# An attention and MLP kernel whose MLP moves from four batches of 448 tokens to runs of 256, 512, 512 and 512 tokens

## The chip, the cores and the metric

The kernel runs on one core of one Trainium2 chip. The metric is the time of one execution on the device in microseconds (us); the time before is the median of three runs. The profile and the trace are of one such execution, taken by the hardware profiler.

## What is computed

Four batches of 12 heads, 448 tokens, head width 64. Softcap attention, then an MLP of 768 to 2048 to 768 on the 1792 tokens:

```python
scores = matmul(q, k.transpose(0, 1, 3, 2)) / sqrt(64)      # (4, 12, 448, 448)
scores = cap * tanh(scores / cap)
attn = exp(scores - max); attn = attn / (sum(attn) + 1e-9)
x = matmul(attn, v).transpose(0, 2, 1, 3).reshape(1792, 768)
h = x @ w_in                                                # (1792, 2048)
out = maximum(0.01 * h, h) @ w_out                          # (1792, 768)
```

q, k, v are float32. w_in and w_out arrive as 8-byte floats and are made into float32 on the chip.

## The kernel before

**Layout.** Everything lies transposed: features on the 128 partitions, tokens along the free dimension. Attention goes by 24 pairs of heads (`plan_pair`, six pairs to a batch); a pair gives one 128-row block of x for the 448 tokens of its batch. The MLP goes by units (`plan_unit`), 34 to a batch: 16 "l1" units, each one 128-row block f of g = leak(h) from the six blocks of x, and 18 "l2" units, each one of six output blocks e from one of three chunks (6, 5, 5 blocks) of g. So each of the four batches has 576 MLP matmuls of 448 columns (line 639).

**Three products for one.** Operands of the MLP are split in a high float32r part and a low rest (`split`, lines 237 to 244: a cast on ScalarE or VectorE and a subtraction on VectorE or GpSimd). A block product is three float32r matmuls: high by high, high by low, low by high. This holds for the weights (each unit's 768 or 640 columns are split again in each batch, line 635), for x (`xh`, `xl`), and for g (`gh`, `gl`). The scores are single float32 matmuls in the first 8 pairs (`fs=8`, lines 481 and 485) and three float32r ones from then on ("parted", lines 475 and 478). The product with v (line 490) is float32 always.

**Weights.** In the first batch each unit's raw 8-byte words are loaded by SP into one of three `wr` buffers, made into float32 in one of three `ws` buffers by two ScalarE steps (lines 624 and 626) and two VectorE steps (628 and 631), stored to a scratch tensor by SP (line 634), and split into one of four `w` buffers. Later batches load `ws` from scratch (line 610) and split.

**Second product.** An l2 unit fills a bank `m` (two banks) with one chunk's product; the first chunk is copied to an accumulator `acc` (line 686), the next two are added on VectorE (line 688); then it is transposed (line 696) and stored.

**Row sums of attention.** Pairs from `tv=4` on are "late": VectorE transposes and reduces `t` (lines 553 and 554) and a small matmul (line 558) folds; the earlier ones use a matmul with ones (line 494).

**Order.** All steps go into a planner (`Plan`). `issue` takes them one by one: the step that can start first by the planner's own costs, ties by a rank. Ranks come from the pair (10 per pair), the unit (`off`, `step`) and many hand-kept shifts (`role`, `pair`, `unit`). Engines run what they get in that fixed order.

Of the kernel before, what the change touches and what calls it, by code (L numbers as in the profile page):

```python
# [22 lines left out]
    kT=2,  # L23
    qT=2,
    pf=6,
    t=1,
    nx=2,
    x=11,
    wr=3,
    ws=3,  # L30
    w=4,
    g=11,
    wl=15,
    wp=6,
    al=7,
    dp=1,
    tv=4,
    fs=8,
    td=1,
# [3 lines left out]
    ps=2.5,  # L43
    pp=7,
    pn=14,
    k1=2,
    wu=16,
    capr=0.5,
    psp=0.05,
    role={'x fold': -295.81, 'x fixed_vx': -299.23, 'x regs': -42.87, 'x cap dma': -211.23, 'x inv': 315.25, 'pair kraw.0 dma zero': -546.92, 'pair qraw.0 zero': -219.17, 'pair kT.0 zero': 57.73, 'pair qT.0 zero': -71.66, 'pair vc.0 dma zero': -347.94, 'pair kb.0 zero': 51.96, 'pair sc.0 zero': -62.66, 'pair sc.1 zero': -60.67, 'pair sc.2 zero': -103.79, 'pair sc.3 zero': -298.93, 'pair pf.0 zero': -156.85, 'pair pf.1 zero': -205.87, 'pair pf.2 zero': -157.62, 'pair pf.3 zero': -489.26, 'pair t.0 zero': -166.0, 'pair po.0 zero': -272.22, 'pair po.1 zero': 319.75, 'pair sums.0 zero': -198.54, 'pair x.0 zero': 43.72, 'pair rt.0 zero': -114.98, 'pair sums.1 zero': -286.23, 'pair x.1 zero': -187.35, 'pair xh.0 zero': -62.77, 'pair xl.0 zero': 379.14, 'pair kraw dma first': -17.18, 'pair qraw dma first': 25.25, 'pair kT first': 241.28, 'pair qT first': 119.93, 'pair vc dma first': -13.95, 'pair kb first': -4.45, 'pair sc first': 21.61, 'pair pf first': -5.02, 'pair t first': -5.18, 'pair po first': 7.52, 'pair sums first': 9.58, 'pair x first': -33.84, 'pair rt first': -21.66, 'pair xh first': -48.48, 'pair xl first': -46.92, 'pair tT first': 13.32, 'pair rs first': -188.37, 'pair tot first': -369.34, 'pair kraw dma': 35.73, 'pair qraw dma': 242.02, 'pair kT': 6.6, 'pair qT': 203.27, 'pair vc dma': 74.48, 'pair kb': 2.15, 'pair sc': -22.89, 'pair pf': 5.21, 'pair t': 8.02, 'pair po': 41.21, 'pair tT': 30.3, 'pair rs': 5.92, 'pair tot': 21.32, 'pair rt': 9.24, 'pair sums': -3.2, 'pair x': -40.44, 'pair xh': -9.56, 'pair xl': 1.21, 'pair kh': -8.73, 'pair kw': -13.73, 'pair qh': 3.89, 'pair qw': -112.56, 'pair fixed_kb': 95.84, 'pair kp': 5.63, 'unit wr dma first': -2.28, 'unit raw first': 0.27, 'unit ws first': -2.37, 'unit scratch dma first': 3.41, 'unit whi first': -11.34, 'unit wlo first': 1.32, 'unit m first': -1.57, 'unit g first': -3.96, 'unit gh first': -19.01, 'unit gl first': -35.21, 'unit acc first': -15.22, 'unit ot first': -312.25, 'unit store dma first': -392.77, 'unit ws dma': -136.88, 'unit whi': -55.41, 'unit wlo': 24.55, 'unit m': -6.45, 'unit g': 9.41, 'unit gh': 273.06, 'unit gl': -123.62, 'unit acc': -15.09, 'unit ot': -213.65, 'unit store dma': -297.05, 'unit kraw': 383.71, 'unit qraw': 313.76, 'unit store': 380.48},  # L50
    pair=[-97.5, -29.54, -10.01, -81.08, -2.56, -7.22, -8.28, 1.67, -3.12, -0.55, -2.65, 1.08, 17.61, 8.32, -39.21, 410.26, -40.91, -16.81, -14.87, 33.57, 95.16, 115.18, 129.54, -71.79],
    unit=[-0.28, -0.21, -0.88, 6.67, -264.45, 3.41, -2.63, -0.84, -1.84, 0.28, 20.81, -3.53, 3.55, -3.25, -1.64, -47.01, -7.36, 5.17, 3.91, -103.33, 4.51, 3.09, -61.42, -11.89, 1.54, -48.36, 9.33, -68.08, -27.04, -5.27, 26.68, -113.13, -88.2, -10.05, 12.8, -156.6, -2.11, -183.67, -162.47, 158.92, -22.97, -152.48, -6.03, -72.99, -38.37, 254.26, 19.64, 15.97, 28.61, 138.2, -309.66, -31.27, -337.13, -7.5, -131.59, 50.82, -44.43, -139.65, 109.84, 27.93, -30.49, -5.42, -7.75, 17.18, -21.48, 90.32, -101.6, 89.32, 60.62, 111.39, -80.62, 162.65, 58.43, 84.77, -48.48, 134.44, 59.07, -210.52, -67.16, 9.79, 12.21, -194.14, -122.58, -150.52, 53.64, -14.13, -35.26, -6.88, 39.73, -132.0, -235.15, -94.07, -115.95, -149.66, -84.77, -83.37, -63.71, -192.65, 151.45, 304.04, 143.0, 46.16, 106.2, 131.92, -65.0, 11.79, 13.3, 34.01, 91.68, 46.33, 129.93, 85.49, 88.82, -179.59, -95.4, 173.17, -320.42, -171.98, -148.32, -76.07, -10.55, 124.57, 325.93, 137.64, 19.88, -79.55, -273.53, 127.53, -258.11, -46.13, -1.94, 80.33, 90.56, -124.12, -123.41, 174.91],
    off=[70, 73, 67, 70],
    step=[1.65, 1.35, 1.65, 1.875],
    pen=0.05,
    pend=0.8,
    phases=[(40.0, {'pool': 1.54, 'dve': 0.21, 'pe': 46.39}), (100.0, {'pool': 0.2, 'dve': 0.47, 'act': 0.31, 'pe': 31.15, 'sp': 28.36}), (200.0, {'pool': 0.53, 'dve': 1.21, 'act': 0.5, 'pe': 6.99}), (1000000000.0, {'pool': 0.78, 'dve': 0.74, 'act': 0.94, 'sp': 11.31})],
    ev=24,
# [7 lines left out]
class Plan:  # L66
# [9 lines left out]
    SWITCH = 20  # L76
# [91 lines left out]

@with_exitstack
def softcap_attention_mlp(  # L170
# [21 lines left out]

    keep = ctx.enter_context(tc.tile_pool(name="keep", bufs=1))
# [7 lines left out]

    def ring(tag, n, shape, dt=F32, pool=const):
        plan.ring(tag, n)
        row = []
        for i in range(n):
            t = pool.tile(shape, dt, name=f"{tag}_{i}", tag=f"{tag}_{i}")
            row.append(t)
        tiles[tag] = row
# [43 lines left out]

    ring("kraw", T["raw"], [P, NB, 32])
    ring("qraw", T["raw"], [P, NB, 32])
    for tag in ("kT", "qT"):
        row = []
        for j in range(2):
            t = const.tile([P, S], F32, name=f"{tag}_{j}", tag=f"{tag}_{j}")
            row.append(t)
        alias(tag, row, [i % 2 if i < T["fs"] else 0 for i in range(B * NP)])  # L260
    ring("kb", 2, [P, P])

# [3 lines left out]
    plan.ring("kp", 1)  # L266
    plan.ring("kw", 1)
    plan.ring("qw", 1)
    block = lambda w: successor(f"kb_{'hl'.index(w)}", [P, P], F32R)
    plan.ring("fixed_kb", 1)  # L270
    ring("vc", 2, [P, 8, D])
    ring("sc", 2, [P, 2, 512], F32, psum)
    late_pair = lambda i: i >= T["tv"]
    n_pairs = B * NP
    two_banks = [psum.tile([P, 512], F32, name=f"po_{j}", tag=f"po_{j}") for j in range(2)]

    alias("po", two_banks, [-1 if late_pair(v // 2) and v % 2 else (v // 2) % 2 if late_pair(v // 2) else v % 2 for v in range(2 * n_pairs)])
# [145 lines left out]
    def plan_pair(i):  # L423
# [426 lines left out]
```

## Time and profile before

| | us |
|---|---|
| median of 3 runs (680.1 to 680.89) | 680.81 |
| span of the profiled execution | 677.4 |
| PE busy | 648.0 |
| VectorE (DVE) busy | 517.1 |
| ScalarE (ACT) busy | 367.0 |
| GpSimd (POOL) busy | 183.4 |

The profiled execution is one of the program; its span runs from the first to the last instruction, and the median of the runs is 3.4 us longer. A busy PE is one with a matmul in flight; it may still be slowed by what it waits for. The views used are: busy time by stretch, groups of instructions, the chain that ended last, and the order in time. The first MLP matmul starts 55 us after the span's start, and the last of batch 0's 576 ends near 246 us; these two times cut the stretches.

### The profile page before, as it was taken

What the parts mean: (1) busy time and instruction counts of PE and PEld (TensorE: products, weight loads), DVE (VectorE), ACT (ScalarE), POOL (GpSimd) and SP (SyncE); (2) the same over time, 40 slices, a digit from 0 to 9 for tenths busy, and PEclk for the clock granted to TensorE, in tenths of its full rate; (3) what the DMA queues carried; (4) which work ended last, traced back from release to release, by engine and by line L of the source; (5) the groups of instructions that cost most, each with busy time, mean ns of one, the idle gap of its engine ahead of it and who ended that gap; (6) DMA issues with size and microseconds to landing.
All of it is one profiled execution on the core that took longest, in us unless ns stands there. A gap on an engine that the chain in (4) does not pass through costs nothing.

```text
span 677.4 us, 9303 instructions
## 1 busy us (share of the span) xinstructions
PE 648.0 (96%) x3208; PEld 510.2 (75%) x3208; DVE 517.1 (76%) x773; ACT 367.0 (54%) x586; POOL 183.4 (27%) x191
## 2 busy tenths in 40 slices
PE   7999999999998999999999999999999999999993
PEld 3334678786765787888656798699879799999993
DVE  3899999999999999538488877954686577465652
ACT  3999998796879843437397614822443113222120
POOL 7425242424633273101266420110011202000001
PEclk8999999999998999999999999999999999999998
DMA  9969899977877677334263355343222266233324
GB/s 134 229 108 223 211 278 233 304 228 200 236 224 219 157 192 155 116 98 118 52 149 79 81 141 119 107 117 102 84 92 78 78 168 156 74 122 108 104 51 73
DMA packets 160104, 98.23 MB, mean 145 GB/s; under 512 B 116529, under 2 KB 141105, under 8 KB 160049
## 3 DMA queue, kind: packets, MB, share of 16 engines
q1 hardware_dynamic: 154192, 91.70, 52.6%
q0 software_dynamic: 3072, 5.51, 4.1%
q10 hardware_dynamic: 2784, 0.34, 0.4%
q8 instruction: 27, 0.44, 0.3%
q14 instruction: 29, 0.23, 0.1%
HBM read 79.43 MB, written 18.09 MB: 144 GB/s over the span
## 4 chain that ended last, share of the span: by engine, by line
PE 62%; DVE 23%; ACT 5%; issue 4%; DMA 3%; POOL 1%; SPq 1%; DVEq 0%; POOLq 0%; ACTq 0%
PE m L639 53%; PE po L490 5%; DVE wr L628 4%; DVE ws L631 3%; PE sc L478 3%; DVE w L244 2%; DMA qraw<-in_q_dram 2%; ACT pf L513 1%; DVE late L679 1%; ACT pf L515 1%; DVE gl L244 1%; DVE t L527 1%; DVE qT_second L244 1%; PE sc L475 1%; DMA wr<-in_moe_w_out_dram 1%
## 5 line engine op out<-in xcount | busy, mean ns | idle before, releaser
L639 PE MATMUL m<-xh,w 128*128 128x448 f32 x768 | 229.9, 372 | 3.4 <-DVE w L244 3.4
L639 PE MATMUL m<-gh,w 128*128 128x448 f32 x768 | 229.3, 369 | 3.9 <-DVE late L688 1.4
L639 PEld LDWEIGHTS m<-xh,w 128*128 128x128 f32 x768 | 144.8, 189 | 24.7 <-DVE w L244 5.5
L639 PEld LDWEIGHTS m<-gh,w 128*128 128x128 f32 x768 | 144.1, 188 | 25.3 <-issue 6.4
L639 PE MATMUL m<-xl,w 128*128 128x448 f32 x384 | 141.1, 367 | 0.0
L639 PE MATMUL m<-gl,w 128*128 128x448 f32 x384 | 140.6, 366 | 0.2 <-DVE gl L244 0.2
L237 ACT CAST w<-ws 128x768 fp32r<-128x768 f32 (+1 forms) x95 | 75.5, 796 | 113.0 <-PE m L639 85.0
L244 DVE TENSOR_TENSOR w<-ws,w 128x768 fp32r<-128x768 f32 (+1 forms) x120 | 114.4, 956 | 19.8 <-ACT w L237 17.8
L513 ACT ACTIVATE pf<-sc 128x896 f32<-128x896 f32 (+1 forms) x90 | 70.7, 823 | 18.2 <-PE sc L478 7.4
L393 POOL DMA_DIRECT2D qraw<-in_q_dram x92 | 58.3, 640 | 74.4 <-DVE gh L241 37.4
L639 PEld LDWEIGHTS m<-xl,w 128*128 128x128 f32 x384 | 72.6, 189 | 6.1 <-issue 0.4
L639 PEld LDWEIGHTS m<-gl,w 128*128 128x128 f32 x384 | 72.1, 188 | 6.3 <-DVE gl L244 0.5
L515 ACT ACTIVATE pf<-pf 128x896 f32<-128x896 f32 (+1 forms) x90 | 74.5, 861 | 0.3
L490 PE MATMUL po<-pf,vc 128*64 128x448 f32 x360 | 73.2, 545 | 0.0
L244 POOL TENSOR_TENSOR gl<-late,gh 128x448 fp32r<-128x448 f32 x14 | 18.0, 1285 | 197.2 <-ACT gh L237 137.2
L674 ACT ACTIVATE late<-m 128x448 f32<-128x448 f32 x51 | 27.6, 543 | 77.4 <-PE m L639 74.4
L679 DVE TENSOR_TENSOR late<-m,late 128x448 f32<-128x448 f32 x64 | 39.4, 618 | 20.0 <-ACT late L674 19.5
L530 POOL TENSOR_TENSOR t<-t,pf 64x448 f32<-64x448 f32 x25 | 34.3, 1372 | 70.9 <-DVE t L527 57.4
L490 PEld LDWEIGHTS po<-pf,vc 128*64 128x64 f32 x360 | 24.0, 136 | 38.6 <-issue 36.1
L688 DVE TENSOR_TENSOR late<-m,late 128x448 f32<-128x448 f32 x48 | 29.6, 618 | 25.3 <-PE m L639 25.0
L241 DVE CAST w<-ws 128x768 fp32r<-128x768 f32 (+1 forms) x41 | 22.0, 539 | 33.6 <-PE m L639 29.7
L244 POOL TENSOR_TENSOR w<-ws,w 128x768 fp32r<-128x768 f32 (+1 forms) x16 | 30.1, 1878 | 59.9 <-PE m L639 24.6
(91 smaller groups left out, 730.3 us busy)
## 6 DMA issues: line engine op xcount, KB each, us to landing
ws<-scratch SPq DMA_DIRECT2D x66, 384.0 KB, 3.1
wr<-in_moe_w_in_dram SPq DMA_DIRECT2D x16, 768.0 KB, 5.6
ws<-scratch SPq DMA_DIRECT2D x36, 320.0 KB, 2.9
scratch<-ws SPq DMA_DIRECT2D x22, 384.0 KB, 5.8
wr<-in_moe_w_out_dram SPq DMA_DIRECT2D x12, 640.0 KB, 5.5
kraw<-in_k_dram SPq DMA_DIRECT2D x96, 56.0 KB, 4.0
qraw<-in_q_dram POOLq DMA_DIRECT2D x92, 56.0 KB, 4.5
vc<-in_v_dram SPq DMA_DIRECT2D x48, 96.0 KB, 4.1
```

The source lines that it names most:

```text
L237: nc.scalar.copy(o, i)
L244: ENG[eng].tensor_tensor(out=o, in0=a, in1=f32(b), op=ALU.subtract)
L393: engine.dma_start(out=t[p0:p0 + 32], in_=src[b, 2 * hp + h, :, 32 * x:32 * x + 32].rearrange("(s i) d -> i s d", i=32),)
L490: nc.tensor.matmul(at("po", 2 * i)[half[j], 0:S], at("vc", i)[0:K, c], pf(g)[:, j if wide(g) == 2 else 0], start=(g == 0), stop=(g == NG - 1))
L513: a = plan.add(r, {"act": ct}, lambda e, sc=sc, g=g: nc.scalar.activation(pf(g), sc(), AF.Tanh, scale=scale_of["tanh"]), vers("sc", [g]) + ...
L515: plan.add(r, {"act": ct + 0.03}, lambda e, g=g: nc.scalar.activation(pf(g), pf(g), AF.Exp, scale=scale_of["exp"]), (), vers("pf", [g]), a ...
L530: plan.add(r + 4, {"dve": 0.65, "pool": 1.3}, lambda e, j=j, g=g: ENG[e].tensor_tensor(out=tt()[half[j], j], in0=tt()[half[j], j], in1=pf( ...
L628: a = plan.add(rank, {"dve": cv}, lambda e: nc.vector.scalar_tensor_tensor(out=word(1), in0=word(1), scalar=-0x80000000, in1=word(0), op0= ...
L639: nc.tensor.matmul(o, l, r, start=(first and m == 0), stop=(last and m == len(mm) - 1))
L674: nc.scalar.mul(at("g", f), ps(), 0.01)
L679: plan.add(rank, {"dve": 0.54}, lambda e: nc.vector.tensor_tensor(out=at("g", f), in0=ps(), in1=at("g", f), op=ALU.max), [("m", m)], [("g" ...
L688: op = plan.add(rank, {"dve": 0.54}, lambda e: nc.vector.tensor_tensor(out=acc(), in0=ps(), in1=acc(), op=ALU.add), [("m", m)], [(tag, b)] ...
```

## The change

MLP units no longer follow batches. `RUNS` cuts the 1792 tokens in runs of 256, 512, 512 and 512 tokens; `PIECES` says where the tokens of each batch go. Run 0 (the first 256 tokens of batch 0) is multiplied in plain float32: x goes to `first`, g to `gr`, and the weights are read from `ws` without a split. Runs 1 to 3 use the three float32r products, with 512 columns to a matmul. x for the coming run stands in `parts` (high and low), what belongs to a later run waits in float32 in `wait` and `tail`, and `plan_parts` splits it. All three chunks of an output block now add up in one bank `m`; `acc` and the VectorE additions are gone, and the transpose reads the bank. The raw weights get up to seven `wr` buffers for the first 24 units (then four), whose space is later that of gh and gl. Scores are float32 in the first 12 pairs (`fs=12`), pairs are late from 6 on (`tv=6`). l2 units go by output block, then chunk. Every rank and shift of the planner has another value. The general path for other caps is not touched.

The core of the diff (of `T`, only what sizes things):

```diff
 T = dict(
     raw=3,
-    x=11,
-    wr=3,
+    banks=11,
+    gt=2,
+    ot=2,
     ws=3,
     w=4,
-    g=11,
+    wrn=24,
+    wrl=4,
-    tv=4,
-    fs=8,
+    fs=12,
+    tv=6,
-    off=[70, 73, 67, 70],
-    step=[1.65, 1.35, 1.65, 1.875],
+    wd=14,
+    xr=-10,
+    off=[66, 130, 195, 255],
+    span=[60, 65, 60, 60],
...
-    SWITCH = 20
+    SWITCH = 9
...
+    RUNS = [(0, 256), (256, 768), (768, 1280), (1280, 1792)]
+    W0, W = 256, 512
+    PIECES = [
+        [(0, 256, "first", 0), (256, 448, "parts", 0)],
+        [(0, 320, "parts", 192), (320, 448, "wait", 0)],
+        [(0, 384, "wait", 128), (384, 448, "tail", 0)],
+        [(0, 448, "wait", 64)],
+    ]
...
+    parts = {w: tile_of(f"x{w}", [P, NE, W], F32R) for w in "hl"}
+    wait = tile_of("wait", [P, NE, W])
+    tail = tile_of("tail", [P, NE, 64])
...
+    NBANK = T["banks"]
+    raw_banks = list(range(1, NBANK - 3))
+    names = ["first"] + ["wr"] * len(raw_banks) + ["gr"] * 3
+    banks = [tile_of(f"bank_{j}", [P, NE, W0], I32 if nm == "wr" else F32) for j, nm in enumerate(names)]
+    def half_of(h):
+        return successor(f"bank_{h // 3}", [P, 3, W], F32R)[:, h % 3]
+    alias("gh", [lambda s=s: half_of(2 * s) for s in range(NSLOT)])
+    alias("gl", [lambda s=s: half_of(2 * s + 1) for s in range(NSLOT)])
...
+        for lo, hi, where, off in PIECES[b]:
+            ...
+            plan.add(rn, {"dve": 0.07 + 1.04e-3 * n}, lambda e, o=o, lo=lo, hi=hi: nc.vector.tensor_tensor(
+                out=o(), in0=at("po", 2 * i)[:, lo:hi], in1=at("sums", 2 * i + 1)[:, lo:hi], op=ALU.mult),
+                [("po", 2 * i), ("sums", 2 * i + 1)], [ver], port=False)
+            if where == "parts":
+                split(rn + 0.5, ...)
...
+    units = [("l1", f) for f in range(NF)] + [("l2", c, e) for e in range(NE) for c in range(NCH)]
...
+    alias("wr", [banks[j] for j in raw_banks], [m % NR if m < wide_raws else NR - T["wrl"] + m % T["wrl"] for m in range(NU)])
...
-            for c in cs:
-                wh, wl = at("w", m)[:, 0, c], at("w", m)[:, 1, c]
-                ops += [(wh, at(hi, src[c])), (wh, at(lo, src[c])), (wl, at(hi, src[c]))]
-            matmuls(ps(), ops, cs[0] == 0, cs[-1] == K - 1)
+            for j in some:
+                c = cs[j]
+                if run == 0:
+                    ops.append((at("ws", m)[:, j], first_x(c) if l1 else first_g(c)))
+                    continue
+                wh, wl = at("w", m)[:, 0, j], at("w", m)[:, 1, j]
+                xh, xl = (parts["h"][:, c], parts["l"][:, c]) if l1 else (at("gh", (run - 1) * NF + c), at("gl", (run - 1) * NF + c))
+                ops += [(wh, xh), (wh, xl), (wl, xh)]
+            for i, (l, r) in enumerate(ops):
+                nc.tensor.matmul(ps(), l, r, start=begins and some[0] == 0 and i == 0, stop=ends and some[-1] == len(cs) - 1 and i == len(ops) - 1)
...
-        _, c, e_ = un
-        tag, acc = f"acc{e_}", lambda: at(f"acc{e_}", b)
-        if c == 0:
-            op = plan.add(rank, {"act": 0.42, "dve": 0.53}, lambda e: copy(e, acc(), ps()), ...)
-        else:
-            op = plan.add(rank, {"dve": 0.54}, lambda e: nc.vector.tensor_tensor(out=acc(), in0=ps(), in1=acc(), op=ALU.add), ...)
+        plan.add(rank, {"dve": turn(size)}, lambda e: nc.vector.transpose(
+            out=at("ot", o)[:, 0:size // 32].rearrange("p s d -> p (s d)"), in_=ps()), [("m", mver)], [("ot", o)], port=False)
```

## Rows read from the trace of the kernel before

**Rows 1.** The page's head and its part 1: span, busy us of each engine.

```profile
span 677.4 us, 9303 instructions
PE 648.0 (96%) x3208; PEld 510.2 (75%) x3208; DVE 517.1 (76%) x773; ACT 367.0 (54%) x586; POOL 183.4 (27%) x191
```

**Rows 2.** Busy time by stretch: PE, PEld, DVE, ACT, POOL, clock, DMA share, GB/s.

```profile
72.00:246.00 174.00, 166.34 (x834) 127.58 (x832) 170.16 (x231) 143.02 (x232) 66.49 (x57) 0.99 0.81 226
246.00:406.00 160.00, 156.80 (x806) 127.16 (x805) 116.71 (x172) 84.47 (x144) 54.20 (x48) 1.00 0.46 114
550.00:667.00 117.00, 116.51 (x575) 107.64 (x574) 71.20 (x112) 24.46 (x38) 5.90 (x6) 1.00 0.40 107
```

**Rows 3.** The same view for line 639 alone: PE, PEld, clock, DMA share, GB/s.

```profile
0.00:55.00 55.00, 0.00 (x0) 0.00 (x0) 0.97 0.96 157
55.00:246.00 191.00, 128.90 (x577) 107.20 (x577) 0.99 0.83 228
246.00:406.00 160.00, 121.41 (x577) 107.39 (x578) 1.00 0.46 114
```

**Rows 4.** The chain that ended last, by time: start us, us, what.

```profile
187.40 0.87 DVE w L244
188.27 0.88 DVE ws L631
...
422.35 1.42 PE sc L478 x12
423.77 3.16 PE po L490 x16
426.92 0.81 PE sc L478 x6
427.73 0.82 PE sc L475 x3
...
440.64 46.40 PE m L639 x228
...
537.53 127.17 PE m L639 x627
```

**Rows 5.** Page part 5, weight loads of the MLP: busy us, mean ns, idle before.

```profile
L639 PEld LDWEIGHTS m<-xh,w 128*128 128x128 f32 x768 | 144.8, 189 | 24.7 <-DVE w L244 5.5
```

**Rows 6.** PE in order of time, float32 matmuls: start us, us, line, tiles, count.

```profile
42.61 1.02 PE L485 MATMUL sc<-qT,kT 64*128 64x448 f32 x4
43.56 1.02 PE L481 MATMUL sc<-qT,kb 128*128 128x448 f32 x2
...
424.12 0.92 PE L490 MATMUL po<-pf,vc 128*64 128x448 f32 x4
...
425.25 0.92 PE L490 MATMUL po<-pf,vc 128*64 128x448 f32 x4
```

**Rows 7.** Groups of instructions on DVE, 0 to 246 us: busy us, mean ns, idle before.

```profile
L628 DVE SCALAR_TENSOR_TENSOR wr<-wr 128x768 int32<-128x768 int32 x22 | 22.6, 1028 | 0.0
L244 DVE TENSOR_TENSOR w<-ws,w 128x768 fp32r<-128x768 f32 x19 | 19.3, 1017 | 0.1
L244 DVE TENSOR_TENSOR gl<-late,gh 128x448 fp32r<-128x448 f32 x15 | 10.7, 725 | 0.0
L244 DVE TENSOR_TENSOR w<-ws,w 128x640 fp32r<-128x640 f32 x10 | 10.0, 1001 | 1.7 <-ACT w L237 1.7
L688 DVE TENSOR_TENSOR late<-m,late 128x448 f32<-128x448 f32 x12 | 7.3, 613 | 0.1
```

**Rows 8.** Lines 626 and 631: count, ns min/median/max, first and last start us.

```profile
L626 ACT ACTIVATE ws<-wr x34: 772/898/1003, 38.7 to 229.0; 128x768 f32<-128x768 f32 x22, 128x640 f32<-128x640 f32 x12
L631 DVE SCALAR_TENSOR_TENSOR ws<-ws,wr x34: 777/946/2476, 50.6 to 233.2; 128x768 int32<-128x768 int32 x22, 128x640 int32<-128x640 int32 x12
```

**Rows 9.** Page part 6, DMA issues: KB each, median us to landing.

```profile
scratch<-ws SPq DMA_DIRECT2D x22, 384.0 KB, 5.8
```

More of the change, by code (lines that the diff above doesn't have):

```diff
@@ L42 @@
     pt=4,
-    ps=2.5,
     pp=7,
     pn=14,
[L46 to L50, printed above, removed]
@@ L59 @@
+    run=[0.0, 0.0, -114.38, -653.71],
+    phases=[(1000000000.0, {'pe': 81.38, 'act': 1.05, 'dve': 2.66, 'pool': 2.36})],
 )
@@ new lines, in plan_parts @@
+    def plan_parts(c, rank):
+        plan.part("run", "", c)
+        first = NE * (c - 1)
+        off = 0
+        if c == 3:
+            off = 64
+            every = [(w, first + n) for w in ("xh",) for n in range(NE)]
+            split(rank, lambda: parts["h"][:, :, 0:off], lambda: parts["l"][:, :, 0:off], lambda: tail, NE * off, [("tail", n) for n in range(NE)],
+                  [("xh", first + n) for n in range(NE)], [("xl", first + n) for n in range(NE)])
+        for n in range(NE):
+            split(rank + n, lambda n=n: parts["h"][:, n, off:], lambda n=n: parts["l"][:, n, off:], lambda n=n: wait[:, n, off:], W - off,
+                  [("wait", NE * (c - 2) + n)], [("xh", first + n)], [("xl", first + n)])
@@ L635, in plan_weights @@
-        split(rank, lambda: at("w", m)[:, 0, 0:n], lambda: at("w", m)[:, 1, 0:n], ws, n * P, [("ws", m)], ("whi", m), ("wlo", m), hi_eng=("act", "dve"))
-    def matmuls(o, mm, first, last):
-        for m, (l, r) in enumerate(mm):
-            nc.tensor.matmul(o, l, r, start=(first and m == 0), stop=(last and m == len(mm) - 1))
-    acc_op = {}
+            split(rank, lambda: at("w", m)[:, 0, 0:n], lambda: at("w", m)[:, 1, 0:n], ws, n * P, [("ws", m)], [("whi", m)], [("wlo", m)])
+            return
@@ new lines, in plan_weights, with store, do @@
+        plan.add(rank, {"dve": cv}, lambda e: nc.vector.scalar_tensor_tensor(
+            out=z(), in0=z(), scalar=3, in1=word(1), op0=ALU.logical_shift_left, op1=ALU.bitwise_or),
+            [("wr", m)], [("ws", m)], after=[a, b])
+        plan.add(rank + 2, {"sp": 0.6}, lambda e: nc.sync.dma_start(out=scratch[m], in_=ws()), [("ws", m)], [(f"scratch{m}", 0)], xfer=0.23 * n)
+    def store(o, run, e_, engines):
+        lo, hi = RUNS[run]
+        def do(e):
+            for r in range(4):
+                (engines[r] if engines else ENG[e]).dma_start(
+                    out=out[lo:hi, e_ * P + 32 * r:e_ * P + 32 * r + 32].rearrange("(s i) d -> i s d", i=32),
+                    in_=at("ot", o)[32 * r:32 * r + 32, 0:(hi - lo) // 32],
+                )
+        return do
@@ new lines, in plan_unit @@
+            if run == 0:
+                return
+            freed = []
+            if run == 1:
+                for h in (2 * f, 2 * f + 1):
+                    j = h // 3
+                    if names[j] == "wr":
+                        freed += [("wr", u) for u in range(NU) if raw_banks[plan.slots["wr"][u]] == j]
+                    elif names[j] == "first":
+                        freed += [("first", c) for c in range(NE)]
+                    else:
+                        lo = NE * (j - (NBANK - 3))
+                        freed += [("gr", u) for u in range(lo, min(lo + NE, NF))]
@@ new lines, in plan_unit @@
+            split(rank, lambda: at("gh", v_), lambda: at("gl", v_), lambda: at("g", v_), size, [("g", v_)], [("gh", v_)], [("gl", v_)], freed=freed)
+            return
+        if not ends:
+            return
+        o = run * NE + un[2]
+        plan.add(rank, {"dve": turn(size)}, lambda e: nc.vector.transpose(
+            out=at("ot", o)[:, 0:size // 32].rearrange("p s d -> p (s d)"), in_=ps()), [("m", mver)], [("ot", o)], port=False)
+        cost, engines = {"sp": 2.1}, None
+        if last_run and un[2] == NE - 1:
+            cost, engines = {"sp": 1.05}, [nc.sync, nc.sync, nc.scalar, nc.scalar]
@@ L719, in softcap_attention_mlp @@
+        plan.add(rank + 1, cost, store(o, run, un[2], engines), [("ot", o)], (), xfer=1.5, port=False)
+    for i in range(n_pairs):
+        plan_pair(i)
+    for run in range(len(RUNS)):
+        if run >= 2:
+            plan_parts(run, T["off"][run] + T["xr"])
+        for n in range(NU):
+            plan_unit(run * NU + n, T["off"][run] + T["span"][run] * n / NU)
     with tc.manual_schedule():
```

413 lines of the change are left out of this document (171 added, 242 removed).

## The prediction, before the change was run

> **What bounds the kernel now.** I read first the busy time by stretch [rows 2], because the page's totals [rows 1] mix two stages. From 72 to 246 us VectorE is busy 170.16 of 174 us, PE 166.34, and DMA 0.81 of its engines' time: nothing there has room. From 246 us on VectorE falls to 116.71 of 160 us, while PE stays at 156.80 of 160 and, at the end, 116.51 of 117. The chain that ended last [rows 4] says the same in another way: at 187 us its steps are VectorE's weight steps, later they are long pieces of PE alone (228 MLP matmuls in 46.40 us, 627 in 127.17 us). So there is a first stage, up to about 246 us, in which the MLP of batch 0 goes as fast as VectorE and its feeders make weights, and a second in which only PE's own work counts.
>
> How much does PE lose in the first stage? At the end 627 matmuls take 127.17 us, 0.2028 us each [rows 4]. At that rate the 577 matmuls between 55 and 246 us would be busy 117.0 us; they are busy 128.90 [rows 3], so 11.9 us are matmuls stretched by waits. PE is also idle 174 - 166.34 = 7.7 us [rows 2]. Together 19.6 us can be won there. From 246 to 406 us the same reckoning gives 121.41 - 117.0 = 4.4 us [rows 3]; I leave that as it is.
>
> **The sum, step by step.** It is made against the profiled span, 677.4 us [rows 1], and 3.4 us are added at the end, the distance of the median 680.81 from that span.
>
> *MLP matmuls.* Before: 4 x 576 = 2304 of 448 columns at 0.2028 us, 467.3 us. After: run 0 has 6 x 16 + 16 x 6 = 192 float32 matmuls of 256 columns, and the three other runs 3 x 576 = 1728 float32r ones of 512. No row has either shape. The float32 rows give a price: the float32 product with v shows two records for a matmul, and two groups of four records, 424.12 and 425.25 us, lie three steps apart [rows 6], so 0.376 us for 448 columns (two of them side by side, each one sweep of a record). By columns that is 0.376 x 256 / 448 = 0.215 us for a record of 256, two records for a matmul: 0.430. For float32r with 512 columns the lower end takes half a float32 record as one sweep: 0.188 x 512 / 448 = 0.215 us. The upper end scales the float32r rate itself: 0.2028 x 512 / 448 = 0.232. Between them decides why 448 columns take 0.2028 and not 0.188. The weight load is 189 ns [rows 5], more than the sweep; so I read the 0.2028 as set by one weight load after the other, which stays as it is when the sweep grows past it. I take 0.216 for both shapes, near the lower end. Then 384 records and 1728 matmuls are 2112 x 0.216 = 456.2 us, a gain of 11.1 us (bounds: 13.2 gained, 16 lost if the 1728 take 0.232).
>
> The Trainium skill has a price for this too: TensorE: Matmul & The Clock Gate, section Back-to-back issue gap, gives an isolated warm matmul N/2.4 + 2.5 ns, thus 215.8 ns for 512 columns and 189.2 for 448. The trace disagrees at 448 (202.8 ns); with the page's figure for 512 the gain would be 11.5 us instead of 11.1.
>
> *Scores.* Pairs 8 to 11 turn from parted to float32. A float32 group starts 0.95 us before the next (42.61 to 43.56 us [rows 6]), four to a pair, 3.80; a parted pair's four groups are 1.42 + 0.81 + 0.82 = 3.05 us [rows 4]. Four pairs lose 4 x 0.75 = 3.0 us on PE (0 to 4). In return each drops its two casts and two subtractions.
>
> *Row sums.* Pairs 4 and 5 take the matmul with ones again: two float32 matmuls side by side, some 0.75 us by the step above, and products with v group by group; +1.5 us for both (0 to 2).
>
> *First stage.* VectorE loses in it the weights' subtractions (19.3 + 10.0 us), g's (10.7) and the additions into `acc` (7.3) [rows 7]: 47 us of some 229 before 246 us, beside half of the leak on 256 columns. The two VectorE and two ScalarE steps that make a weight stay, and so do their loads and the scratch stores: all 34 units, now for 256 tokens instead of 448. So VectorE is no longer the bound, but the ring of three `ws` buffers (rival 2) and the DMA (rival 3) move up behind it. I take a third of the 19.6 us as won, 6.5 (bounds: all of it won; or none won and more lost, as rival 2 reckons). A third, since two other limits stand close behind VectorE.
>
> *Second product.* In later runs the 36 additions and 18 copies leave VectorE and ScalarE, which are not late there [rows 2]: nothing on the path. A new wait: the bank `m` of an output block is now held for 48 matmuls, some 10 us, before the transpose frees it; the other bank takes the next block meanwhile, and the transpose of 512 columns needs under a us. Nothing. At the very end one addition of 0.613 us [rows 7] before the last transpose goes: -0.6.
>
> *Joins.* A run needs x of all pairs of its last batch: run 1 pairs up to 11, run 2 up to 17, run 3 up to 23. While run r is multiplied the next six pairs are computed; their PE time is about 6.2 us a pair [rows 4] beside 124 us of MLP, ScalarE and VectorE have the room they have from 246 us on [rows 2]. The split of `wait` in `plan_parts` adds six casts and six subtractions on 448 to 512 columns in the second half of a run, less than the split of all of x before. I cost it at nothing; what hides it is 18 l2 units of matmuls, some 60 us; without that cover it would be about 6 x 1.5 = 9 us a run.
>
> *Queues.* SP issues the raw loads up to 14 ranks ahead instead of 8, past the loads of k, q and v of the pairs around rank 50. In the first 55 us the DMA share is 0.96 [rows 3]; a pair that comes 1 to 3 us later is possible there, inside the range.
>
> Sum: 677.4 - 11.1 + 3.0 + 1.5 - 6.5 - 0.6 = 663.7 us of span, 667 us of time.
>
> **The rivals.**
>
> *1. The first stage loses all its stalls.* For: VectorE is the releaser on the chain there [rows 4] and sheds 47 us. Against: PE, ScalarE (143 of 174 us) and DMA are nearly as full. The sum with 19.6 instead of 6.5: 654 us.
>
> *2. The `ws` ring sets the pace of run 0, and the kernel is slower.* Before, a split freed `ws` and four `w` buffers stood between the weights and PE. Now PE reads `ws` itself, and a buffer is held from its first write through line 631, its scratch store and its matmuls. Line 631 runs 34 times from 50.6 to 233.2 us [rows 8]: 5.5 us a unit. PE needs for run 0 only 192 x 0.432 = 83 us, and 6 pairs at 3.80 + 3.16 and the changes of shape, some 48: 131 us, 3.9 a unit. Each hold is at least 0.90 + 1.03 + 0.95 us of steps [rows 7, 8] and a store of 5.8 [rows 9], so three buffers allow 3.2 us a unit if nothing waits; with VectorE as crowded as before, 5.5. PE can fill about 2.5 pairs ahead (three raw, two `vc` buffers), 16 us. Against the 654 us of rival 1, idle is 34 x pace - 131 - 16; the kernel gets slower than before from 27 us of idle, that is from 5.1 us a unit. At 5.4 it is 36.6 us of idle and 691 us.
>
> *3. The DMA fills up.* Before 246 us the engines worked 0.96 x 55 + 0.83 x 191 = 211 us [rows 3], of which I estimate 16 for pairs from 12 on and for outputs. Nearly all the rest is still to be moved, now by about 190 to 200 us. It would end at about 203, and PE can fill part of the difference with pairs; none of the 19.6 us is then won, and a few more are lost: 677 us, with a part of this case inside 0.2% of the time before.
>
> *4. A 512-column matmul costs by its columns, 0.232 us.* Against: the float32 rows, where a sweep takes 0.188. Price 1728 x 0.016 = 27.6 us: 695 us.
>
> **How the numbers follow.** Forecast 0.45, rival 1 0.17, rival 2 0.20, rival 3 0.14, rival 4 0.04. The forecast's own range is 660 to 674 us (matmul price 0.215 to 0.218, a third of the stalls give or take 5 us). The range for 8 in 10, 653 to 692, leaves out the better half of rival 1 and the upper parts of rivals 2 and 4. A difference of 0.2%, 1.4 us, is about what a measurement of this kernel can tell from none. Faster: 0.45 + 0.17 + 0.09 of rival 3 = 0.71; the same 0.06 (0.05 of rival 3 and a part of the rest); slower 0.23.
>
> **What would show it.** In the changed profile: the MLP of runs 1 to 3 at 0.215 to 0.218 us a matmul where nothing waits (0.232 is rival 4); run 0's float32 records at 0.215; line 631 34 times at 4.0 to 4.7 us a unit (above 5.1 is rival 2); VectorE under 0.9 of the stretch in which run 0 runs; the DMA share there below 0.95 (above, rival 3); run 0 ending at about 195 to 205 us, and from there on PE without gaps. Should PE stand idle for more than 10 us at the start of runs 1 to 3, the joins that I cost at nothing have failed. Wrong altogether would be a first stage that is not shorter by some 40 us: the later runs have 1536 tokens instead of 1344, and alone they are 22 us longer than batches 1 to 3 were.

## The result, and the profile after

The kernel is slower: 688.05 us in the median (687.44 to 689.41), a ratio of 1.0115 to the kernel before, interval 1.0097 to 1.0132. The forecast was 667 us, faster; the range held the time, the sign was wrong.

The page's head and part 1 of the kernel after (span; busy us of each engine), against [rows 1]:

```profile
span 685.5 us, 8696 instructions
PE 659.3 (96%) x2992; PEld 473.6 (69%) x2992; DVE 432.1 (63%) x636; ACT 376.1 (55%) x592; POOL 62.1 (9%) x76
```

The change did what it says. VectorE is down from 517.1 to 432.1 us, GpSimd from 183.4 to 62.1, there are 607 instructions fewer. PE is busy longer, 659.3 against 648.0 us, ScalarE too (376.1 against 367.0), and PE is what sets the end. Of the 121 us that GpSimd has less, 41 are loads of q: it issued 92 of 96 before and issues 28 now, SP the other 64 beside its own.

Busy time by stretch of the kernel after (length; PE, PEld, DVE, ACT, POOL, clock, DMA share, GB/s), against [rows 2, 3]:

```profile
0.00:55.00 55.00, 46.12 (x178) 18.42 (x178) 33.28 (x63) 41.37 (x61) 17.23 (x36) 1.00 0.95 168
55.00:152.00 97.00, 90.15 (x396) 50.97 (x396) 83.78 (x128) 76.94 (x120) 17.77 (x18) 0.98 0.93 241
152.00:249.00 97.00, 93.57 (x480) 62.97 (x480) 92.08 (x146) 78.84 (x132) 16.53 (x15) 0.98 0.87 222
250.00:400.00 150.00, 150.00 (x682) 119.32 (x681) 89.42 (x122) 70.51 (x114) 2.73 (x2) 1.00 0.43 114
400.00:550.00 150.00, 150.00 (x693) 115.39 (x692) 79.36 (x109) 65.19 (x103) 7.76 (x5) 1.00 0.36 96
550.00:678.00 128.00, 127.94 (x565) 105.63 (x564) 52.41 (x68) 42.22 (x63) 0.00 (x0) 1.00 0.34 92
```

Two things are to be seen. From 250 us on PE has hardly a gap (150.00 of 150, 150.00 of 150, 127.94 of 128 us), so whatever is lost there is in the length of PE's own work. And the first stage did not get shorter: run 0's matmuls go from 65.5 to 247.2 us, where batch 0's went from 55.1 to 242.7 (the next MLP matmul starts at 248.7 and at 245.95 us; the 246 us at which the stretches of before were cut are that start).

The chain that ended last (start us, us, what), against [rows 4]:

```profile
27.61 0.48 SPq L590
28.14 8.97 DMA bank<-in_moe_w_in_dram
...
49.30 6.16 DMA bank<-in_moe_w_in_dram
...
110.40 5.77 DMA bank<-in_moe_w_in_dram
116.19 0.94 ACT bank L608
...
120.53 5.34 DMA bank<-in_moe_w_in_dram
125.89 0.91 ACT bank L608
...
477.89 51.23 PE m L660 x225
...
547.42 64.16 PE m L660 x282
```

Early in the stage the chain's long pieces are now raw weight loads of 5 to 9 us (line 590 issues them); late in the kernel they are pieces of PE, as before, but 225 matmuls take 51.23 us and 282 take 64.16: 0.2277 and 0.2275 us each, with short waits in them. Where two float32r matmuls stand directly behind each other, starts lie 226.8 ns apart in the mean. The forecast had 216.

The weights' last VectorE step in the kernel after (line 615, line 631 before; count, ns min/median/max, first and last start us), against [rows 8], and run 0's float32 matmuls with the weight load of a later run (part 5: busy us, mean ns, idle before), against [rows 5]:

```profile
L615 DVE SCALAR_TENSOR_TENSOR ws<-ws,bank x34: 782/948/1356, 59.3 to 240.4; 128x768 int32<-128x768 int32 x22, 128x640 int32<-128x640 int32 x12
L660 PE MATMUL m<-bank,ws 128*128 128x256 f32 x384 | 92.9, 391 | 4.3 <-DVE ws L615 3.5
L660 PEld LDWEIGHTS m<-bank_second,w 128*128 128x128 f32 x864 | 161.7, 188 | 35.0 <-ACT pf L495 0.7
```

34 units in 181.1 us are 5.49 us a unit (33 steps), as slow as before (5.53). The 384 records of run 0 are the two records of 192 matmuls; back to back their starts lie 216.0 ns apart, as forecast.

The end (order in time: start us, us, engine, line, what), kernel after:

```profile
671.79 0.72 DVE L703 STREAM_TRANSPOSE ot<-m 128x512 f32<-128x512 f32 x1 [5.87 <-PE m L660]
678.59 0.72 DVE L703 STREAM_TRANSPOSE ot<-m 128x512 f32<-128x512 f32 x1 [6.08 <-PE m L660]
679.34 2.02 ACTq L625 DMA_DIRECT2D out_dram<-ot  x2
```

The end of the kernel before, the same view:

```profile
664.72 0.63 DVE L688 TENSOR_TENSOR late<-m,late 128x448 f32<-128x448 f32 x1 [2.95 <-PE m L639]
665.38 0.65 DVE L696 STREAM_TRANSPOSE kraw<-late 128x448 f32<-128x448 f32 x1
666.55 0.62 DVE L688 TENSOR_TENSOR late<-m,late 128x448 f32<-128x448 f32 x1 [0.53 <-PE m L639]
667.21 0.65 DVE L696 STREAM_TRANSPOSE qraw<-late 128x448 f32<-128x448 f32 x1
667.88 4.60 SPq L702 DMA_DIRECT2D out_dram<-qraw  x2
```

Before, the last two output blocks ended 1.8 us apart, and their eight stores went out by GpSimd, SP and ScalarE: SP's last one stood in its queue for 3.9 us, until a store that ScalarE had issued at 667.89 us and whose semaphore it uses again had landed (672.10). It was issued at 672.16 us and landed at 674.56, 8.0 us behind the last matmul (666.51). After, with output blocks done one by one, the last two transposes lie 6.8 us apart and the last store lands at 683.15, 4.6 us behind the last matmul (678.55).

**The account.** The span grew by 8.1 us (677.4 to 685.5), where the forecast took 13.7 from it. I split each trace by the starts of PE's matmuls: pitches from one MLP matmul directly to the next (2249 of them, 473.1 us, before; 2055, 469.8 us, after), and all other time. "Bare price" is the number of matmuls times their pitch where nothing waits: 2304 x 0.2028 = 467.3 before, 384 x 0.216 + 1728 x 0.2268 = 474.8 after.

| us | forecast | measured |
|---|---|---|
| MLP matmuls at their bare price | -11.1 | +7.5 |
| waits between one MLP matmul and the next (17.0 before, 7.5 after) | -6.5 | -9.5 |
| all else on PE: attention, changes of shape, waits there | +4.5 | +14.1 |
| behind the last matmul (10.9 before, 6.9 after) | -0.6 | -4.0 |
| sum | -13.7 | +8.1 |

The first line alone is 18.6 of the 21.8 us between forecast and result. The second and third together give what the stage won and lost beside that: 9.6 us more than costed on attention and the changes of shape, 3.0 more won between MLP matmuls, thus 6.6 us worse than the forecast.

By time the same 8.1 us lie as follows. The first MLP matmul comes 10.4 us later (65.5 against 55.1); from there to the first MLP matmul of the next run or batch it is 7.6 us less (183.2 against 190.8), from there to the end of the last matmul 9.3 more (429.8 against 420.6), behind it 4.0 less. So 10 of the 14.1 us in the third line stand before the first MLP matmul: PE's pitches inside attention there sum up to 63.3 us against 53.3, for nearly the same work (207 and 197 pitches, five pairs' products with v in both).

### The profile page after: what moved, and what is told of

Same layout as the page of the kernel before. It is cut to its first block, busy times and chain, and to the rows that moved or that the text cites. A ratio compares the mean times of both kernels' runs of the same rounds, so it can differ in the third digit from the quotient of the medians.

```text
span 685.5 us, 8696 instructions
## 1 busy us (share of the span) xinstructions
PE 659.3 (96%) x2992; PEld 473.6 (69%) x2992; DVE 432.1 (63%) x636; ACT 376.1 (55%) x592; POOL 62.1 (9%) x76
## 4 chain that ended last, share of the span: by engine, by line
PE 78%; DMA 9%; DVE 4%; SPq 4%; ACT 3%; issue 2%; DVEq 0%
PE m L660 64%; PE po L478 7%; DMA bank<-in_moe_w_in_dram 5%; PE sc L467 4%; SPq L396 2%; DVE bank L612 1%; ACT pf L495 1%; DMA bank<-in_moe_w_out_dram 1%; PE sc L464 1%; DMA vc<-in_v_dram 1%; ACT pf L497 1%; ACT bank L608 1%; DMA qraw<-in_q_dram 1%; PE sc L473 1%; DVE ws L615 1%
## 5 line engine op out<-in xcount | busy, mean ns | idle before, releaser
L660 PE MATMUL m<-bank_second,w 128*128 128x512 f32 x864 | 198.8, 390 | 0.1
L660 PEld LDWEIGHTS m<-bank_second,w 128*128 128x128 f32 x864 | 161.7, 188 | 35.0 <-ACT pf L495 0.7
L660 PE MATMUL m<-xh,w 128*128 128x512 f32 x576 | 181.5, 391 | 0.0
L660 PEld LDWEIGHTS m<-xh,w 128*128 128x128 f32 x576 | 108.1, 188 | 27.2 <-issue 2.9
L660 PE MATMUL m<-xl,w 128*128 128x512 f32 x288 | 112.2, 389 | 0.0
L660 PE MATMUL m<-bank,ws 128*128 128x256 f32 x384 | 92.9, 391 | 4.3 <-DVE ws L615 3.5
L660 PEld LDWEIGHTS m<-bank,ws 128*128 128x128 f32 x384 | 71.9, 193 | 25.1 <-DVE ws L615 6.1
L660 PEld LDWEIGHTS m<-xl,w 128*128 128x128 f32 x288 | 54.1, 188 | 10.9
L683 DVE TENSOR_TENSOR g<-m,g 128x512 f32<-128x512 f32 x48 | 33.0, 687 | 39.7 <-ACT g L678 39.5
L473 PE MATMUL sc<-qT,kT 64*128 64x448 f32 x144 | 34.6, 576 | 9.0 <-ACT pf L495 8.8
L247 DVE TENSOR_TENSOR bank_second<-g,bank_second 128x512 fp32r<-128x512 f32 x46 | 31.7, 689 | 16.4 <-ACT bank_second L240 16.1
```

What stands on the lines that cost most here:

```text
L247: ENG[eng].tensor_tensor(out=o, in0=a, in1=f32(b), op=ALU.subtract)
L473: nc.tensor.matmul(sc[:, j, 0:S], at("kT", i)[half[j], tile_keys(j, g)], at("qT", i)[half[j]], start=True, stop=True)
L660: nc.tensor.matmul(ps(), l, r, start=begins and some[0] == 0 and i == 0, stop=ends and some[-1] == len(cs) - 1 and i == len(ops) - 1)
L683: plan.add(rank, {"dve": 0.07 + 1.04e-3 * size}, lambda e: nc.vector.tensor_tensor(out=g(), in0=ps(), in1=g(), op=ALU.max), [("m", mver)], ...
```

## The experiments

**What sets a matmul's price.** Run 3 of the kernel after, in several shapes. It changes how many columns, weight columns (outputs) and weight rows each matmul takes, one output block in float32:

```diff
+    L1_COLS = [512, 480, 448, 416, 384, 320, 256, 128]
+    L2_SHAPE = [(512, P, P, False), (512, P, 64, False), (512, P, 32, False), (448, P, 64, False), (512, 64, P, False), (512, P, P, True)]
...
+                    l, r = l[0:rows, 0:outs], r[0:rows, 0:min(cols, size)]
+                    if plain:
+                        l, r = f32(l), f32(r)
```

> The changed kernel, but the matmuls of run 3 take other shapes, so part of run 3's product is left out: l1 units 512, 480, 448, 416, 384, 320, 256 or 128 columns by turn; l2 units of output block 0 as before, block 1 with 64 and block 2 with 32 output rows, block 3 with 64 output rows and 448 columns, block 4 with 64 of 128 contraction rows, block 5 in float32 with 512 columns. Measured so far: 448 columns 202.8 ns a matmul in the kernel before, 512 columns 226.8 ns in the changed one. Theory A, a fixed part: the sweep at 2.4 columns a ns and some 14 ns more whatever the width: 480 columns 214, 448 201, 416 188, 384 174, 320 148, 256 121 ns; 64 or 32 output rows with 512 columns still 227. Theory B, sweep and weight load share one rate (columns plus 128 weight columns at 2.83 a ns): 480 215, 448 203, 416 192, 384 181, 320 158, 256 136, 128 90 ns; 64 output rows with 512 columns fall to 213 (the sweep), with 448 to 187. Theory C, the one of the prediction, a floor of one weight load after the other near 203 ns: 448 and all narrower ones stay at about 200 ns. Float32 with 512 columns: two records of 427 to 430 ns by all three if only float32r has the extra, 441 by A if every record has it.

Its time is 702.79 us and says nothing by itself, since the shapes differ. The pitches do. PE, for each width in order of time (start us, us, line, tiles, shape, count): of the repeating pattern two starts of the same kind, three matmuls apart. Among those of 256 columns stands one of their weight loads (PEld):

```profile
575.84 0.39 PE L671 MATMUL m<-xl,w 128*128 128x512 f32 x1
576.07 0.62 PE L671 MATMUL m<-xh,w 128*128 128x512 f32 x2
576.52 0.39 PE L671 MATMUL m<-xl,w 128*128 128x512 f32 x1
...
583.80 0.36 PE L671 MATMUL m<-xl,w 128*128 128x448 f32 x1
584.00 0.57 PE L671 MATMUL m<-xh,w 128*128 128x448 f32 x2
584.40 0.36 PE L671 MATMUL m<-xl,w 128*128 128x448 f32 x1
...
569.58 0.19 PEld L671 LDWEIGHTS m<-xl,w 128*128 128x128 f32 x1
569.69 0.28 PE L671 MATMUL m<-xl,w 128*128 128x256 f32 x1
569.81 0.40 PE L671 MATMUL m<-xh,w 128*128 128x256 f32 x2
570.05 0.28 PE L671 MATMUL m<-xl,w 128*128 128x256 f32 x1
...
565.84 0.28 PE L671 MATMUL m<-xl,w 128*128 128x128 f32 x1
565.96 0.39 PE L671 MATMUL m<-xh,w 128*128 128x128 f32 x2
566.18 0.28 PE L671 MATMUL m<-xl,w 128*128 128x128 f32 x1
```

576.52 - 575.84 = 0.68 us for three matmuls of 512 columns, 0.60 for 448, 0.36 for 256, 0.34 for 128. The means over all undisturbed pitches of the run:

| columns | ns a matmul | columns x 0.417 ns | rest |
|---|---|---|---|
| 512 | 226.8 | 213.3 | 13.5 |
| 480 | 216.8 | 200.0 | 16.8 |
| 448 | 202.6 | 186.7 | 15.9 |
| 416 | 186.6 | 173.3 | 13.3 |
| 384 | 173.6 | 160.0 | 13.6 |
| 320 | 146.7 | 133.3 | 13.4 |
| 256 | 119.7 | 106.7 | 13.0 |
| 128 | 110 to 114 | 53.3 | 57 to 61 |

The 0.417 ns a column is the slope of these numbers themselves, (226.8 - 119.7) / 256 = 0.418, and a column per cycle at the clock's level of 2.4 GHz, which was granted there (clock 1.00 from 550 to 690 us). So a float32r matmul costs its sweep and 13 to 17 ns more, at every width down to 256. With 64 weight columns 512 columns take 230.2 ns, with 32 of them 231.9, with 64 weight rows 227.7, while the load itself falls from 188 to 134, 108 and 184 ns: the rest does not follow the weight load. That the load sets 0.2028 at 448 columns, on which the forecast chose its price, is refuted: at 256 columns, with the same load of 188 ns, matmuls follow each other every 119.7 ns. Nor do sweep and load share one rate, which wanted 158 ns at 320 columns and 136 at 256. Only at 128 columns does the price leave the line: 110 to 114 ns, but for 60 ns once at the start of each unit. A float32 record of 512 columns takes 429 ns, of 256 columns 216.0: two sweeps and only 2 to 3 ns. The forecast took its 512-column price from float32 rows, which don't carry the larger rest.

**The price against the time.** All 1728 matmuls of runs 1 to 3 on 484 of their 512 columns, in the same order:

```diff
+    def shape_of(run, un):
+        return 484, P, P, False
...
+                    l, r = l[0:rows, 0:outs], r[0:rows, 0:min(cols, size)]
```

> The changed kernel with 484 of 512 columns in each matmul of runs 1 to 3, the width at which a float32r matmul should take the 216 ns of the prediction (28 columns of each product are left out; the warm-up writes whole banks). The order of the instructions is the same. If the price of the 512-column matmul is what the forecast missed, the time falls by 1728 x 10.8 ns = 18.7 us to about 669 us, beside the 667 forecast. If the later runs are not bound by PE after all, or the first stage gives the lost time anew, it falls by less than 12 us.

672.89 us (671.67 to 674.42), 0.987 of the kernel before (0.9832 to 0.9908). The pitch is 218.6 ns, close to the 216 that the forecast had put on 512 columns. The saving in bare price, 1728 x 8.2 ns = 14.2 us, is what MLP pitches lose (469.8 to 455.6 us) and most of the 15.2 us by which the median is under that of the kernel after (16.7 by the two ratios to before). So what a matmul costs less passes to the end, and nothing takes its place: at about the forecast's price the kernel would have been faster, and the 18.6 us of the account's first line decide the sign.

**DMA in the first stage.** Half of each unit's raw words are loaded from the eighth unit on:

```diff
-        nc.sync.dma_start(out=at("wr", m)[:, 0:n], in_=src.bitcast(I32).rearrange("(c p) f -> p c f", p=P))
+        some = n if m < NR else n // 2
+        nc.sync.dma_start(out=at("wr", m)[:, 0:some], in_=src.bitcast(I32).rearrange("(c p) f -> p c f", p=P)[:, 0:some])
```

> The changed kernel with only half of the raw weight words loaded from unit 7 on (the other half of a buffer keeps what an earlier unit left, so the weights are wrong); all steps and their order stay. If the DMA engines set the pace of run 0, the pace of line 615 falls from 5.5 us a unit to 4.6 to 5.1 and the time by 5 to 12 us. If the ring of weight buffers, or the order itself with PE behind it, sets the pace, the time stays within 2 us.

682.41 us (681.16 to 683.02), 1.0009 of before (0.9992 to 1.0027): 5.6 us under the kernel after by the medians, 7.2 by the ratios to before. Busy time by stretch in this run (columns as above), and its line 616, which is 615 of the kernel after:

```profile
55.00:152.00 97.00, 93.85 (x420) 53.47 (x418) 88.36 (x140) 81.68 (x129) 18.73 (x19) 0.98 0.79 199
152.00:249.00 97.00, 94.35 (x489) 63.13 (x489) 93.40 (x144) 81.15 (x135) 17.58 (x15) 1.00 0.67 173
L616 DVE SCALAR_TENSOR_TENSOR ws<-ws,bank x34: 780/948/1347, 60.4 to 234.4; 128x768 int32<-128x768 int32 x22, 128x640 int32<-128x640 int32 x12
```

The DMA share falls from 0.93 and 0.87 to 0.79 and 0.67, and PE works 3.7 us more in the first 97 us, 0.8 in the second. The pace is 5.27 us a unit instead of 5.49, not the 4.6 to 5.1 expected, though the time is in the range expected with it. So the loads do hold the stage, by 5 to 7 us, and are not its only limit. With them halved the units still come at 5.27, and VectorE (88.36 and 93.40 of 97) and PE (93.85 and 94.35) are both nearly full; which of them then sets the pace this run does not tell.

**The ring of three `ws` buffers.** Twice. First four buffers, the second `ot` buffer given up for it; the planner keeps the shifts of the kernel after and makes another order from them:

```diff
-    ot=2,
-    ws=3,
+    ot=1,
+    ws=4,
```

> The changed kernel with four ws buffers instead of three (and one ot instead of two, to make room); the planner makes another order. If the ring of three sets the pace of run 0, the pace falls to 4.2 to 5.0 us a unit and the time by 5 to 12 us. If the DMA engines do, the time stays within 3 us, and the DMA share of the first stage stays above 0.9.

709.52 us (708.7 to 712.58), 1.0423 of before (1.0376 to 1.047). The pace is 5.34 us a unit (51.0 to 227.1), yet the whole is 21 us slower than the kernel after; the order is another one, from shifts that were set for three buffers, so it tells nothing of the ring. Then four buffers with the order of the kernel after, for which the planner goes on counting three; some units then read another unit's weights:

```diff
-    ring("ot", T["ot"], [P, W // 32, 32])
-    ring("ws", T["ws"], [P, NE, P])
+    alias("ot", [tile_of("ot_0", [P, W // 32, 32])] * T["ot"])
+    ring("ws", T["ws"] + 1, [P, NE, P])
+    plan.ring("ws", T["ws"])
```

> The changed kernel with four real ws buffers, while the planner goes on counting three, so that every engine has the same instructions in the same order (one ot buffer instead of two, to make room). If the ring of three holds up run 0 as it runs, instructions that waited for a buffer start earlier and the time falls by 5 us or more. If the DMA engines and the written order set the pace, it stays within 2 us of 688.

691.41 us (689.06 to 692.53), 1.0165 of before (1.0132 to 1.0198): no gain over the kernel after, 3.4 us more. The pace is 5.38 us a unit (60.5 to 238.0) instead of 5.49. At this order the ring isn't what holds the stage, or by little; what the single `ot` buffer costs in this run isn't separated. Whether an order made for four buffers could use them stays open.

**Run 0 in float32r.** x, g and weights of run 0 are split too, three products of 256 columns instead of a float32 one; to make room there are three raw buffers instead of seven; shifts set anew:

```diff
-                    if run == 0:
-                        ops.append((at("ws", m)[:, j], first_x(c) if l1 else first_g(c)))
-                        continue
...
+                    of = first_x if l1 else first_g
+                    xh, xl = (of("h", c), of("l", c)) if run == 0 else (parts["h"][:, c], parts["l"][:, c]) if l1 else (at("gh", (run - 1) * NF + c), at("gl", (run - 1) * NF + c))
```

> The changed kernel with run 0 in float32r too: weights, x and g of the first 256 tokens are split and multiplied in three products (three raw buffers instead of seven; the planner's shifts are set anew). By the widths measured, 256 columns take 119.7 ns in float32r, so PE's work falls by 192 x (432 - 3 x 119.7) ns = 14.0 us. If PE's work alone sets the time: 674 us. If VectorE and ScalarE set the pace of the first stage, the 34 casts and 34 subtractions of weights (0.8 and 0.95 us each) that come back there cost as much as PE gains or more: 685 to 700 us.

699.1 us (699.02 to 704.63), 1.0299 of before (1.0248 to 1.0351). By the table above three products of 256 columns cost 0.359 us where one float32 product costs 0.432, so PE's work falls by 192 x 0.073 = 14.0 us. Its busy time does fall, to 651.5 us. The stretches show why the time rises (columns as above):

```profile
55.00:152.00 97.00, 82.53 (x454) 52.17 (x453) 86.74 (x136) 84.11 (x139) 19.12 (x16) 0.91 0.89 237
152.00:249.00 97.00, 86.60 (x553) 62.09 (x552) 94.14 (x132) 85.40 (x141) 26.62 (x17) 0.96 0.84 219
```

PE is idle 25 of 194 us (10 in the kernel after), VectorE and ScalarE are busier, and the granted clock is 0.91 and 0.96. So here the cheaper products brought nothing. That their split is the dearer part is likely but not shown: the raw buffers, the order and the granted clock differ too, and I don't split the 11 us among them.

**The second product alone.** The kernel before, with nothing of the change but output blocks added up in one bank, units by output block; batches of 448 and the weights' split stay. The buffers follow from it (16 g tiles instead of 11, 7 x tiles instead of 11, 8 pf tiles). Shifts set anew:

```diff
-    units = [("l1", f) for f in CHUNKS[0] + CHUNKS[1][:1]]
-    for c in range(NCH):
-        units += [("l2", c, e) for e in range(NE)]
-        units += [("l1", f) for f in sum(CHUNKS[c + 1:c + 2], [])[1:] + sum(CHUNKS[c + 2:c + 3], [])[:1]]
+    units = [("l1", f) for f in range(NF)] + [("l2", c, e) for e in range(NE) for c in range(NCH)]
...
-                matmuls(ps(), ops, cs[0] == 0, cs[-1] == K - 1)
+                matmuls(ps(), ops, begins and cs[0] == 0, ends and cs[-1] == K - 1)
```

> The kernel before with one part of the change alone: l2 units by output block, the three chunks of a block summed in one bank, no acc, the transpose from the bank (16 g tiles instead of 11, 7 x tiles instead of 11, 8 pf tiles; the planner's shifts are set anew). PE's work stays that of before, 2304 matmuls at 203 ns. By the account made after the result (price of 512 columns and the float32 run cost 7.5 us, the end gains 3.9), this part alone is faster than before by about 4 us at the end, plus what the 7.3 us of additions free in the first stage: 670 to 677 us. If the gain at the end came from the 512-token runs and not from the order of the l2 units, 680 to 682.

680.61 us (678.92 to 682.96), 1.0012 of before (0.9996 to 1.0027): the same. Its control is the kernel before with the shifts set anew in the same manner and nothing else:

```diff
-    role={'x fold': -295.81, 'x fixed_vx': -299.23, ...},
+    role={'pair fixed_kb': 23.38, 'pair kT': 69.32, ...},
...
-    MM = 0.2045
+    MM = 0.2035
```

> The kernel before with nothing but its role, pair, unit and phases shifts set anew, in the way they were for e6_run0_f32r, e7_one_bank and e8_replanned, and the planner's price of an MLP matmul at 0.2035 as in e7_one_bank; the computation is unchanged. It is the control for e7_one_bank (680.61 us, no better than before though its last store lands 3.4 us nearer to the last matmul and VectorE has 54 additions less to do). Theory P: shifts set anew in this way cost some us against the order of the kernel before, and the one bank gave them back: 684 to 692 us, and e7_one_bank's part is worth 4 us or more. Theory N: the new order costs nothing and the one bank is worth nothing but what its order takes back: 679 to 682 us.

683.08 us (681.7 to 685.38), 1.005 of before (1.0024 to 1.0077): between the two expectations. So an order set anew costs some 0.5% here, and against that control the one-bank kernel is about 0.4% faster, 2.6 us (the two intervals just touch). The two have different orders, and orders alone differ by as much, so the 2.6 us are not shown to be the bank's; the distance of the last store from the last matmul is 3.1 us less. The order in time of the one-bank kernel:

```profile
667.22 0.37 PE L626 MATMUL m<-gh,w 128*128 128x448 f32 x1
667.63 0.65 DVE L678 STREAM_TRANSPOSE ot<-m 128x448 f32<-128x448 f32 x1 [9.09 <-PE m L626]
668.30 1.65 SPq L684 DMA_DIRECT2D out_dram<-ot  x2
```

Its last store lands 4.6 us behind the last matmul (667.59 to 672.24), as in the kernel after; in the control it is 7.7 (669.79 to 677.48), and there SP's last store stands in its queue as in the kernel before (to 675.34 us). That the additions taken from VectorE brought anything more is not shown.

**The order of the kernel after, for the right price.** The planner's price of a 512-column matmul set to what was measured, shifts set anew:

```diff
...
-    MMW = 0.2170
+    MMW = 0.2268
```

> The changed kernel, ordered anew with the measured price of a 512-column matmul (0.2268 instead of 0.2170 us in the planner; shifts set anew). If the loss comes from PE's work, as the account says, it stays at 683 to 690 us. If it came from an order made for a wrong price, it falls below 680.

695.96 us (693.45 to 699.05), 1.0242 of before (1.0203 to 1.0281), 7.9 us worse than the kernel after and outside both expectations. Its pitches from one MLP matmul to the next sum up to 470.1 us (469.8 in the kernel after) and those inside attention to 167.4 (167.3); at the changes between the two it spends 44.5 us (39.4). So PE's own work is the same, and more time goes at the changes. The right price with shifts set anew did not win the loss back; since shifts set anew made the kernel before slower too, this doesn't say what the best order for 0.2268 would give. Why one order is better than another is not settled by these runs.

## Why the prediction was wrong, step by step

**MLP matmuls: the failed step.** The prediction had both ends, 0.215 from half a float32 record and 0.232 from the float32r rate scaled, and chose the lower because "I read the 0.2028 as set by one weight load after the other". The price is 0.2268, near the upper end, and the reading is refuted by the 119.7 ns at 256 columns beside a 188 ns load. The better reading was in the rows: 0.2028 and a sweep of 0.188 differ by 15 ns, and adding those 15 ns to 0.215 gives 0.230. The term was -11.1 us and is +7.5. With it alone put right the sum is 682.3 us of span, 685.7 of time, slower.

Run 0's half of the step held: 216.0 ns a record against 0.216.

The figure of the Trainium skill (TensorE: Matmul & The Clock Gate, section Back-to-back issue gap) would have given 215.8 ns at 512 columns. The runs have 226.8 for float32r, and 216.0 and 429 for float32 records of 256 and 512 columns, each of two sweeps. For such a record two sweeps and the 2.5 ns of that section of the Trainium skill, counted once, make as an estimate 215.8 and 429.2 ns, within 1 ns of these. So the figure fits the float32 records and not the float32r matmuls; the prediction had seen it miss at 448 and still took a price beside it at 512.

**First stage.** A third of 19.6 us was to be won. Between MLP matmuls 9.5 us were won; the 9.6 us beyond the costs given lie in attention, changes of shape and waits there, most of them before the first MLP matmul (see Queues), so nothing was won net. The units came at 5.49 us, not at the 4.0 to 4.7 named as the sign, and run 0 ended at 247 us, not at 195 to 205: by the prediction's own last test, wrong altogether here. VectorE was at 0.86 and 0.95 of the two stretches, where under 0.9 was named. It was freed of 47 us of weights', g's and the additions' work and filled up again with attention: when the next run's first MLP matmul started (248.7 us), 18 pairs' products with v were done, where before 14 were (245.95). That fits the unmoved pace not costing what rival 2 reckoned: these pairs need not be done later, and of the last stretch attention and the changes take 40.4 us where they took 70.4. The prediction let PE fill about 2.5 pairs ahead of the six that run 0 needs; by the stage's end it was twelve ahead.

**Scores and row sums** (+4.5): not seen apart; they lie in the +14.1, which holds waits too.

**Second product:** nothing on the path, as costed; what the new order by output block does to the stores was not in the sum, and the end moved by 3.4 us more than the -0.6. The one-bank run shows that part by itself (4.6 against 7.7 us).

**Joins:** nothing, as forecast. PE has hardly a gap from 250 us on, at the start of no run.

**Queues: a second miss.** 1 to 3 us were allowed and none stood in the sum; the first MLP matmul starts at 65.5 us instead of 55.1, after hardly more work on PE. The DMA share of the first 55 us is 0.95, where it was 0.96, so the engines are no fuller. The prediction had the raw loads go out earlier; in the trace SP issues the first at 27.61 us, before at 18.11. They stand on the chain (28 to 37 us, 49 to 55 us), and the first weight is made 8.7 us later (line 615 at 59.3 us, line 631 at 50.6). What this costs at the end isn't shown: PE has pairs to do meanwhile (46 of the first 55 us busy, 90 of the next 97), and the kernel ordered anew for 0.2268, which issues its first raw load at 18.1 us, starts its MLP 4.7 us earlier than the kernel after (60.8 us) behind the same number of matmuls and yet ends later.

**Rivals.** 1 (all stalls won) did not come. 2 came with its pace and without its price. 3 (DMA) came in part: halving the raw loads gives 5 to 7 us, and the share was 0.93 and 0.87, not full. 4 (0.232, chance 0.04) was nearest to the truth in the price and had by far the lowest chance; 0.2268 is two thirds of the way from 0.215 to 0.232. That the range held 688 us is luck: it reached so far mostly for rival 2, and what made the time was the price. Rival 2's lower bound of 3.2 us a unit is 2.9 by its own terms (8.68 us over three buffers); nothing in the forecast rests on it.

**What stays open:** where the 13 to 17 ns of a float32r matmul come from; what paces the first stage once the loads are light (in the half-load run VectorE and PE are nearly full, ScalarE at 0.84 and the DMA at 0.79 and 0.67 of the two stretches); what the late first MLP matmul costs at the end; and why orders with nearly equal work differ by 8 to 21 us. None of the variants that compute the whole beat the kernel before.

## What to carry to other kernels

A price for a shape that the trace doesn't show is scaled from rows of the same data type, with the fixed part kept: two widths of one type give the slope and the rest, and a row of another type gives neither. Before a cause is given for a price ("the weight load sets it"), look for what it forbids; here one run at 256 columns refuted it. And an engine that is relieved in a full stage is filled by the next work in the queue: ask how far ahead that work can go before counting the relief, or the idle time, as time.

## What the runs showed of the hardware

A float32r matmul took 0.417 ns a column and 13 to 17 ns more, at 256 to 512 columns; at 512 columns it was 14 to 19 ns more with 64 or 32 weight columns or 64 weight rows; a float32 record took two sweeps and 2 to 3 ns. At 128 columns it took 110 to 114 ns. Weight loads recorded at 188 ns did not keep matmuls from following each other every 119.7 ns. Three float32r products of 256 columns cost 0.359 us, one float32 product 0.432. A store of SP stood in its queue for 3.9 us until another queue's store with the same semaphore had landed.
